# Attention and two gated layers in one kernel: in feature blocks 7 to 9 of the first layer, the middle token tile's halves get seven block products for eight

## The chip, the cores and the metric

The kernel runs on one core of a Trainium2 chip. The metric is the device time of one execution in microseconds (us); the median of 3 runs of the kernel before is 554.49 us (554.37 to 554.83). Besides these there is one profiled execution, which has a time of its own; all rows shown below come from it.

The engines are named as in the profile: PE is the matrix engine (PEld its loads of weights), DVE the vector engine, ACT the scalar engine, POOL the engine that issues accumulating transfers here, SP the one that issues plain loads and stores.

## The reference

Three stages follow one another; the output of each is the input of the next. The tokens are 2 batches of 768, 1536 in all; the model width is 512.

```python
# attention with a decaying state, 8 heads of 64
for t in range(S):
    state = gamma[None, :, None, None] * state + np.einsum('bhd,bhe->bhde', k[:, :, t], v[:, :, t])
    y[:, :, t] = scale * np.einsum('bhd,bhde->bhe', q[:, :, t], state)
x = np.ascontiguousarray(y.transpose(0, 2, 1, 3)).reshape(B * S, H * D)
# first layer: d_model 512, d_ff 1536
x = (x @ w_a) * (x @ w_b) @ w_out
# second layer: d_model 512, d_ff 2048
h = x @ w_in
out = np.maximum(0.01 * h, h) @ w_out2
```

## The kernel before

**Number format.** A float32 factor is kept as two parts, high (`h` at the end of a name) and low (`l`), and a product is three matmuls, high by high, high by low and low by high. One helper, `mm3`, issues all of them, so every matmul of the kernel stands on line 261, 262 or 263. The high part is made by a cast (CAST in the rows), the low part by a subtraction on DVE, or, for the a blocks, by a negated copy on ACT and an accumulating transfer that POOL issues.

**Tiles and blocks.** The 1536 tokens lie in three token tiles of 512: 0 and 2 are the outer ones, 1 is the middle one. The 1536 hidden features of the first layer lie in 12 blocks f of 128 features. Blocks 0 and 1 are plain. In blocks 2 to 11 (`FAST`), `seven_for_eight` takes the two outer tiles and the pair (a, b) of weight blocks together: seven block products take the place of eight, in the manner of Strassen and Winograd. They need sums of x over the outer tiles (S1 to S4, with forms `s10h` and so on), made once, and sums of the weight blocks (`ta`, `tb`, made in `sub_items` from the kept tiles of the block). The middle tile is computed plainly into the banks `pa` and `pb`: x1 by a and x1 by b, 24 matmuls of 512 columns in a block. The outer seven products go into the PSUM banks `top`, `left` and `mid`, 42 matmuls of 512 columns.

In the second layer the same is done with pairs of feature blocks, and there from the third pair on the function `seven_in_all` also gives the middle tile its seven products: its two halves of 256 tokens take the part of the outer tiles, into the half banks `intop`, `inleft` and `inmid`, 42 matmuls of 256 columns in the place of 24 of 512.

**Order of the work.** PE's stream is written out block by block. Each block is a Python generator: its first product (x10 and x11 by the next a block) is issued in the tail of the block before (`next(now)`), and its last four products stand behind that (`next(before, None)`). Behind these stand 12 matmuls of the product with w_out (`blk`, its operands called `forma`), from block 4 on.

The other engines' work is of two sorts. What a product needs at its end (a copy out of its bank, an addition) is called where it stands in the code: `s1` is the copy of the first sum out of `top` (written `h<-top`, tile h of token tile 0), `u3` the later copy out of `top` into the tile h of token tile 2, `c22` the addition of `mid` to it. All else (rounding the weights, splitting them, forming operands for w_out) lies in a queue of small items, each with a cost in microseconds that the author gave it; `pump(us)` runs items until their costs add up to `us`, `until(...)` runs them until something is there. This decides the order in which ACT and DVE get their instructions. Each engine takes its instructions in the order given.

On ACT the rounding of one weight tile begins with three instructions (the lines 330, 332 and 334, called the triple below); it ends with three on DVE.

The result of a product stays in its bank until its reader on ACT or DVE has read it, and PE may write that bank again only then. In a fast block `top` is filled by x00 and x01 with a, is read by `s1`, and is filled on by `top<-s20,tb`.

## Time and profile before

| | us |
|---|---|
| median of 3 runs | 554.49 (554.37 to 554.83) |
| the profiled execution | 553.83 |
| its span in the profile | 552.0 |
| PE busy | 547.2 (99%) |
| DVE busy | 468.3 (85%) |
| ACT busy | 394.1 (71%) |
| POOL busy | 162.5 (29%) |

The profiled execution took 0.66 us less than the median, and 1.83 us of it lie outside the span. The chain of work that ended last is PE for 96% of the span and DVE for 3%. The busy times of PE overlap from one matmul to the next (a matmul of 512 columns is shown with 0.39 us although the next begins 0.23 us later), so what counts for PE is the distance from start to start.

### The profile page before, as it was taken

To read this page: it belongs to the slowest core of one execution; us is meant where nothing else is said; L and a number is where in the kernel's file an instruction comes from. 1 tells how busy PE (TensorE), PEld (TensorE's weight loads), DVE (VectorE), ACT (ScalarE), POOL (GpSimd) and SP (SyncE) were. 2 spreads that over 40 slices of the span, in tenths; PEclk is the share of its full clock that TensorE was granted. 3 is DMA by queue.
4 is the path that set the end of the run, shared out by engine and by line. 5 is a ranking of instruction groups with operands and counts; after the bars stand their busy time and mean duration, and the time that the engine had idled before them with its cause. 6 is when DMAs were issued, how large, how long until landed. Compare 5 with 4: busy or idle time off the path is not lost.

```text
span 552.0 us, 10803 instructions
## 1 busy us (share of the span) xinstructions
PE 547.2 (99%) x3850; PEld 465.9 (84%) x3850; DVE 468.3 (85%) x1000; ACT 394.1 (71%) x821; POOL 162.5 (29%) x211
## 2 busy tenths in 40 slices
PE   9999999999999999999999999999999999999997
PEld 6878888888888888788888888888888888888886
DVE  4978968898898898899799798998989688999862
ACT  4877477787779888867768367879878777686800
POOL 3425101113232331277520320332533456700000
PEclk9999999999999999999999999999999999999999
DMA  8999835548687887899991451967979899974111
GB/s 315 354 349 242 217 96 134 155 133 207 182 260 233 247 224 249 272 299 240 237 248 39 83 110 39 245 200 230 330 222 279 259 306 259 221 168 125 58 58 57
DMA packets 51782, 112.93 MB, mean 205 GB/s; under 512 B 6224, under 2 KB 13648, under 8 KB 51728
## 3 DMA queue, kind: packets, MB, share of 16 engines
q1 hardware_dynamic: 28800, 69.16, 38.1%
q0 software_dynamic: 22784, 43.00, 35.5%
...
q14 instruction: 24, 0.20, 0.1%
...
## 4 chain that ended last, share of the span: by engine, by line
PE 96%; DVE 3%; ACT 0%; issue 0%; DVEq 0%
PE blk L262 12%; PE blk L261 12%; PE blk L263 12%; PE top L261 6%; PE top L262 6%; PE top L263 6%; PE mid L261 3%; PE pa L261 3%; PE mid L262 3%; PE mid L263 3%; PE pa L263 3%; PE pa L262 3%; PE pb L261 3%; PE pb L263 3%; PE pb L262 3%; PE left L263 1%
## 5 line engine op out<-in xcount | busy, mean ns | idle before, releaser
L262 PE MATMUL blk<-form,form 128*128 128x512 f32 (+1 forms) x224 | 75.8, 339 | 0.0
L261 PE MATMUL blk<-form,form 128*128 128x512 f32 (+1 forms) x224 | 75.6, 337 | 0.0
L263 PE MATMUL blk<-form,form 128*128 128x512 f32 (+1 forms) x224 | 75.3, 336 | 0.0
L177 DVE TENSOR_TENSOR form<-g,form 128x512 fp32r<-128x512 f32 x112 | 57.8, 554 | 1.8 <-DMA out<-c 0.9
L171 ACT CAST form<-g 128x512 fp32r<-128x512 f32 x112 | 52.5, 513 | 7.5 <-DMA g<-g 5.0
L262 PE MATMUL blk<-forma,forma 128*128 128x512 f32 (+1 forms) x168 | 56.9, 338 | 0.0
L261 PE MATMUL blk<-forma,forma 128*128 128x512 f32 (+1 forms) x168 | 56.7, 337 | 0.0
L263 PE MATMUL blk<-forma,forma 128*128 128x512 f32 (+1 forms) x168 | 56.4, 336 | 0.0
L261 PEld LDWEIGHTS blk<-form,form 128*128 128x128 f32 x224 | 42.5, 190 | 5.3
L262 PEld LDWEIGHTS blk<-form,form 128*128 128x128 f32 x224 | 42.5, 190 | 4.7
L263 PEld LDWEIGHTS blk<-form,form 128*128 128x128 f32 x224 | 42.3, 189 | 4.8
L177 DVE TENSOR_TENSOR forma<-h,forma 128x512 fp32r<-128x512 f32 x84 | 43.1, 554 | 2.2 <-ACT forma L171 0.7
L171 ACT CAST forma<-h 128x512 fp32r<-128x512 f32 x84 | 38.8, 511 | 1.4 <-DMA h<-h 1.4
L150 POOL DMA_DIRECT2D h<-h x33 | 32.9, 1151 | 12.4 <-DVE forma L177 6.0
L787 POOL DMA_DIRECT2D farg<-g x26 | 16.1, 635 | 66.9 <-ACT g L1516 42.1
L261 PEld LDWEIGHTS blk<-forma,forma 128*128 128x128 f32 x168 | 31.9, 190 | 4.0
L262 PEld LDWEIGHTS blk<-forma,forma 128*128 128x128 f32 x168 | 31.9, 190 | 3.5
L263 PEld LDWEIGHTS blk<-forma,forma 128*128 128x128 f32 x168 | 31.7, 189 | 3.6
L787 POOL DMA_DIRECT2D farh<-h x19 | 10.9, 576 | 74.8 <-DVE h L1030 50.5
L177 DVE TENSOR_TENSOR form<-wq,form 128x256 fp32r<-128x256 f32 x56 | 23.6, 421 | 7.8 <-ACT form L171 7.7
L171 ACT CAST form<-wq 128x256 fp32r<-128x256 f32 x56 | 22.7, 406 | 5.8 <-DVE wq L193 3.3
L150 POOL DMA_DIRECT2D g<-farg x22 | 22.8, 1242 | 8.9 <-DVE form L177 5.4
...
## 6 DMA issues: line engine op xcount, KB each, us to landing
...
farg<-g POOLq DMA_DIRECT2D x26, 256.0 KB, 4.5
g<-farg SPq DMA_DIRECT2D x26, 256.0 KB, 7.7
...
g<-farg POOLq DMA_DIRECT2D x20, 256.0 KB, 8.5
```

The lines of the kernel that those rows point to most:

```text
L150: queue.append((0.0, lambda piece=piece: self.nc.gpsimd.dma_start(self.A(*d[1:], j)[piece], self.A(*x1[1:], j)[piece], accum_op=ALU.add)))
L171: nc.scalar.copy(h, src)
L177: nc.vector.tensor_sub(*todo.pop(0))
L261: nc.tensor.matmul(ps, w[0], x[0], start=first, stop=False, skip_group_check=more)
L262: nc.tensor.matmul(ps, w[0], x[1], start=False, stop=False, skip_group_check=more)
L263: nc.tensor.matmul(ps, w[1], x[0], start=False, stop=last, skip_group_check=more)
L787: nc.gpsimd.dma_start(self.far[t, f], self.tiles[t, f])
```

## The change

In blocks 7, 8 and 9 of the first layer (`INNER1`) `fast(f)` calls `seven_in_all`, which now takes its inputs, its sums and the pumps as arguments. The middle tile's plain 24 matmuls of 512 columns become 42 of 256 columns there. Over the whole kernel PE loses 72 matmuls of 512 columns and gains 126 of 256.

What this needs besides:
- The sums of x over the halves of the middle tile. In block 3 four tiles `xm` are loaded from the high parts of x (SP), and the low parts are added to them by accumulating transfers (POOL), 256 KB each. Eight sums of 256 columns on DVE and four splits (a cast on ACT, `mx0h` to `mx3h`, and a subtraction on DVE) are given out over the blocks 3 to 6 by `SHARE`, and the rest, the splits of `mx2` and `mx3`, is queued when block 7 begins.
- The middle tile's ends: copies out of the half banks on ACT, four additions or products more on DVE.
- In blocks 7 to 9 only the upper half of the b block is split, since only that half is multiplied by itself. The high casts of `tb7`, `ta7`, `tb8` and `tb9` are on DVE (on ACT before).
- The stores of finished h tiles of these blocks wait in a list until the low part of the a block two further on has been issued (`landed`, `waiting`).
- The pump behind each w_out product is 0.5 in these blocks for 2.0; the pumps within a block come from `DUE` and a tuple.
- The kernel's functions `lend` and `recall` are moved, and do the same.

```diff
+DUE = {7: 2.4, 8: 1.8, 9: 1.0}
+SHARE = {3: 3, 4: 3, 5: 4, 6: 2}
+INNER1 = range(7, 10)
...
     def enqueue_split(key, keep=False, far=False):
-        part = slice(QT, TT) if key[0] == "wi" and key[1] % 2 and key[1] > 2 * INNER else slice(0, TT)
+        half = key[1] % 2 and key[1] > 2 * INNER if key[0] == "wi" else key[0] == "b" and key[1] in INNER1
+        part = slice(QT, TT) if half else slice(0, TT)
...
                 nc.gpsimd.dma_start(weights[key][1], src, accum_op=ALU.add)
+                landed.add(key)
+                while waiting:
+                    hs.send(*waiting.pop(0))
...
-                (nc.vector.tensor_copy if k[0] == "wi" else nc.scalar.copy)(weights[t][0], kept[k])
+                own = k[0] != "wi" and k[1] not in INNER1 or k[0] == "a" and k[1] > INNER1[0]
+                (nc.scalar.copy if own else nc.vector.tensor_copy)(weights[t][0], kept[k])
...
-    def seven_in_all(ka, kb, ends, inner, bent):
+    def seven_in_all(ka, kb, X, S, M, flush, ends, inner, bent, pace):
...
-        product(top, ka, 0, [y[0, 0], y[0, 1]], True, False)
+        product(top, ka, 0, [X[0, 0], X[0, 1]], True, False)
         s1(top)
         bent(1)
-        product(left, ka, 1, [y[0, 2], y[0, 3]], True, False)
+        product(left, ka, 1, [X[0, 2], X[0, 3]], True, False)
+        pump(pace[3])
         c11(left)
         left = bank("inleft")[:, 0:QT]
         product(left, ka, 1, token(X1, 0), True, False)
         mc11(left)
-        while ym:
-            spare.pop(0)[1]()
-        pump(2.7)
+        flush()
+        pump(pace[4])
         until(lambda: ta in weights and ka not in kept)
...
     def fast(f):
...
+        def mc12(ps):
+            add(um[0], um[0], ps)
+            mul(part(0), part(0), um[0])
+            half_done()
+
+        def mc21(ps):
+            nc.vector.scalar_tensor_tensor(part(1), part(1), -1.0, ps, op0=ALU.mult, op1=ALU.mult)
+            half_done()
...
+        if f in INNER1:
+            return seven_in_all(("a", f), ("b", f), x, S, inner, flush, (
+                lambda top: nc.scalar.copy(h[0, f], top),
+                lambda left: add(h[0, f], h[0, f], left),
+                uu,
+                lambda mid: nc.scalar.copy(h[2, f], mid),
+                lambda top: add(h[2, f], h[2, f], top),
+                c21, c12,
+            ), (
+                lambda ps: in_copy(part(0), ps),
+                lambda ps: add(part(0), part(0), ps),
+                muu,
+                lambda ps: in_copy(part(1), ps),
+                lambda ps: add(part(1), part(1), ps),
+                mc21, mc12,
+            ), lambda n: None, (0.4, 0.8, 0.8, 1.5, DUE.get(f, 3.6), 5.6 - DUE.get(f, 3.6)))
...
+    def inner_x():
...
+        for j in range(2):
+            for op, d, p, q in (
+                (minus_both, (2 + j, 1), (j, 1), (2 + j, 1)), (sub, (j, 1), (j, 0), (j, 1)),
+                (add, (j, 0), (j, 0), (2 + j, 1)), (add, (2 + j, 0), (2 + j, 0), (j, 0)),
+            ):
+                yield 0.42, lambda op=op, d=d, p=p, q=q: op(piece(*d), piece(*p), piece(*q))
+        for n in range(4):
+
+            def high(n=n):
+                MX[n] = slots.new(F32R, f"mx{n}h"), slots.new(F32R, f"mx{n}l")
+                nc.scalar.copy(MX[n][0], xm[n])
...
+            yield 0.05, high
+            yield 0.69, low
...
     def make_products(f):
         for n in MADE[f]:
             until(lambda: n in z.forms)
             z.product(n)
-            pump(2.0)
+            pump(0.5 if f in INNER1 else 2.0)
...
+    sums_x = list(inner_x())
     before = None
     for f in range(NBLOCK, FF1):
+        if f == INNER1[0]:
+            queue.extend(sums_x)
+        if f == NBLOCK + 1:
+            for kc in range(KC):
+                xm[kc] = slots.new(F32, f"xm{kc}")
+                nc.sync.dma_start(xm[kc], as32(x[1, kc][0]))
+                nc.gpsimd.dma_start(xm[kc], as32(x[1, kc][1]), accum_op=ALU.add)
...
+        for _ in range(SHARE.get(f, 0)):
+            queue.append(sums_x.pop(0))
```

**What stands where, first place: ACT between the last copy out of `top` in block 6 and `s1` of block 7.** In the names, a8 and b8 are weight blocks, `h26` is tile h of token tile 2 in block 6 (so `h26<-top` is `u3` of block 6), `h07<-top` is `s1` of block 7, `wo4` is a block of w_out. In the kernel before, ACT's program has this behind the two casts of `tb7` and `ta7`:

```order
L1044 COPY h26_227_1987<-top_2069 128x512
L330 ACTIVATE a8_244_2173<-raw_a8_2009 128x512
L332 ACTIVATE sl22_2174<-raw_a8_2009 128x512
L334 ACTIVATE sl22_2174<-raw_a8_2009 128x512
```

Behind that come the other two instructions of a8's triple and the triple of b8, and then, up to `s1`:

```order
L406 CAST a8h_246_2195<-a8_244_2173 128x512
L413 ACTIVATE a8l_247_2196<-a8h_246_2195 128x512
L330 ACTIVATE wo4_248_2213<-raw_wo4_2086 128x512
L332 ACTIVATE sl24_2214<-raw_wo4_2086 128x512
L334 ACTIVATE sl24_2214<-raw_wo4_2086 128x512
L171 CAST forma3_2237<-wo3_232_2035 128x256
L171 CAST forma3_2234<-h03_179_1515 128x512
L171 CAST forma3_2236<-h13_180_1516 128x256
L406 CAST b8h_249_2245<-b8_245_2189 128x512
L1040 COPY h07_241_2163<-top_2249 128x512
```

In the changed kernel the copy `h26<-top` is followed by a copy out of `intop`, which holds the first product of block 7's middle tile, and by two casts of the sums of x:

```order
L1102 COPY h26_229_2011<-top_2092 128x512
L1056 COPY h17_244_2191<-intop_2193 128x256
L1128 CAST mx2h_246_2201<-xm2_180_1521 128x512
L1128 CAST mx3h_248_2211<-xm3_181_1524 128x512
L333 ACTIVATE a8_250_2215<-raw_a8_2033 128x512
```

Behind that come again the rest of a8's triple and the triple of b8, and then:

```order
L410 CAST a8h_252_2256<-a8_250_2215 128x512
L417 ACTIVATE a8l_253_2257<-a8h_252_2256 128x512
L333 ACTIVATE wo4_254_2265<-raw_wo4_2109 128x512
L335 ACTIVATE sl24_2266<-raw_wo4_2109 128x512
L337 ACTIVATE sl24_2266<-raw_wo4_2109 128x512
L174 CAST forma3_2273<-wo3_234_2059 128x256
L174 CAST forma3_2270<-h03_182_1527 128x512
L174 CAST forma3_2272<-h13_183_1528 128x256
L1082 COPY h07_243_2190<-top_2279 128x512
```

The two casts of `tb7` and `ta7` are gone from ACT, a copy out of `intop` and the casts of `mx2` and `mx3` stand ahead of the triples, and the cast of b8 stands behind `h07<-top` now.

**Second place: DVE in block 11**, around `c22` (`h211<-h211,mid`, the addition of `mid` to tile h of token tile 2). Before:

```order
L177 TENSOR_TENSOR forma6_3035<-h10_163_1389,forma6_3035 128x256
L177 TENSOR_TENSOR forma7_3059<-wo1_201_1704,forma7_3059 128x256
L177 TENSOR_TENSOR forma7_322_3057<-h01_120_937,forma7_321_3056 128x512
L1045 TENSOR_TENSOR h211_310_2904<-h211_310_2904,mid_3012 128x512
L177 TENSOR_TENSOR forma7_3058<-h11_164_1399,forma7_3058 128x256
L177 TENSOR_TENSOR forma8_3070<-wo2_216_1853,forma8_3070 128x256
```

In the changed kernel:

```order
L354 ISA wq2_317_3129<-wq2_317_3129,sl44_3130 128x1024
L180 TENSOR_TENSOR forma6_3157<-wo0_189_1577,forma6_3157 128x256
L1103 TENSOR_TENSOR h211_308_3004<-h211_308_3004,mid_3106 128x512
L180 TENSOR_TENSOR forma6_319_3155<-h00_100_699,forma6_318_3154 128x512
L180 TENSOR_TENSOR forma6_3156<-h10_163_1389,forma6_3156 128x256
L1040 TENSOR_TENSOR h111_307_3003<-h111_307_3003,pb_3107 128x512
```

Before, one subtraction of 256 columns and one of 512 stand directly ahead of `c22`; now only one of 256 columns does, and that of 512 columns stands behind it.

## Rows read from the trace of the kernel before

**Rows 1.** Busy times in stretches: blocks 7, 9, and pair 3 of layer two.

```profile
core 0: us, PE busy (x) PEld busy (x) DVE busy (x) ACT busy (x) POOL busy (x), PEclk, DMA share, GB/s
...
155.92:172.98 17.06, 17.06 (x80) 14.23 (x79) 14.95 (x30) 13.72 (x26) 4.95 (x7) 1.00 0.78 220
...
190.04:207.10 17.06, 17.06 (x80) 14.23 (x79) 15.85 (x32) 14.34 (x28) 5.33 (x8) 1.00 0.85 234
...
345.75:362.49 16.74, 16.74 (x99) 14.75 (x98) 15.76 (x36) 14.46 (x30) 4.75 (x6) 1.00 0.80 211
```

**Rows 2.** PE in order of time, blocks 6 and 7: start, duration, instruction.

```profile
141.61 0.39 PE L261 MATMUL pa<-x12h,a6h 128*128 128x512 f32 x1
...
142.97 0.39 PE L261 MATMUL top<-s20h,tb6h 128*128 128x512 f32 x1
...
148.41 0.39 PE L261 MATMUL pb<-x12h,b6h 128*128 128x512 f32 x1
...
149.77 0.39 PE L261 MATMUL pa<-x10h,a7h 128*128 128x512 f32 x1
...
160.03 0.39 PE L261 MATMUL top<-s20h,tb7h 128*128 128x512 f32 x1
```

**Rows 3.** PE in order of time, second layer: two products of 256 columns.

```profile
348.49 0.28 PE L261 MATMUL inleft<-y10h,wi4h 128*128 128x256 f32 x1
...
349.21 0.28 PE L261 MATMUL intop<-m2h,twi5h 128*128 128x256 f32 x1
```

**Rows 4.** ACT in order of time, from `u3` of block 6 on.

```profile
148.61 0.59 ACT L1044 COPY h<-top 128x512 f32<-128x512 f32 x1 [1.52 <-PE top L263]
149.09 0.67 ACT L330 ACTIVATE a<-raw_a 128x512 f32<-128x512 f32 x1
...
152.77 0.59 ACT L406 CAST a8h<-a 128x512 fp32r<-128x512 f32 x1
...
155.77 0.38 ACT L171 CAST forma<-wo 128x256 fp32r<-128x256 f32 x1
156.05 0.92 ACT L171 CAST forma<-h 128x512 fp32r<-128x512 f32 x2
156.88 0.61 ACT L406 CAST b8h<-b 128x512 fp32r<-128x512 f32 x1
157.51 0.59 ACT L1040 COPY h<-top 128x512 f32<-128x512 f32 x1
```

**Rows 5.** PE in order of time, block 11.

```profile
234.10 0.39 PE L263 MATMUL top<-x23h,ta11l 128*128 128x512 f32 x1
234.59 0.50 PE L261 MATMUL mid<-s40h,b11h 128*128 128x512 f32 x1
```

**Rows 6.** DVE in order of time, block 11, in the same stretch.

```profile
232.73 0.42 DVE L177 TENSOR_TENSOR forma<-wo,forma 128x256 fp32r<-128x256 f32 x1 [1.02 <-ACT forma L171]
233.25 0.69 DVE L177 TENSOR_TENSOR forma<-h,forma 128x512 fp32r<-128x512 f32 x1
233.86 0.68 DVE L1045 TENSOR_TENSOR h<-h,mid 128x512 f32<-128x512 f32 x1
234.46 0.42 DVE L177 TENSOR_TENSOR forma<-h,forma 128x256 fp32r<-128x256 f32 x1
234.79 0.42 DVE L177 TENSOR_TENSOR forma<-wo,forma 128x256 fp32r<-128x256 f32 x1
```

**Rows 7.** SP's queue in block 3, in order of time.

```profile
88.37 0.33 SPq L306 DMA_DIRECT2D raw_b<-in_wab  x1
```

**Rows 8.** POOL in block 3, in order of time.

```profile
90.83 0.58 POOL L787 DMA_DIRECT2D farh<-h  x1 [10.72 <-DVE h L1030]
91.59 0.85 POOL L414 DMA_DIRECT2D a4l<-a  x1 [0.17 <-issue]
```

**Rows 9.** Transfers issued from 85 to 102 us: size, us to landing.

```profile
a4l<-a POOLq DMA_DIRECT2D x1, 256.0 KB, 5.7
```

**Rows 10.** PE in order of time, block 3: where a4's low part is used.

```profile
101.14 0.39 PE L263 MATMUL pa<-x10h,a4l 128*128 128x512 f32 x1
```

109 lines of the change are left out of this document (74 added, 35 removed).

## The prediction

> **What bounds the kernel now.** I read the page first: the chain of waits is PE almost alone. Then the table of stretches, one line per block [rows 1]: in a fast block PE is busy for the whole 17.06 us, the granted clock is 1.00, DVE is busy for 14.95 to 15.85 and ACT for 13.72 to 14.34. So no wait can be taken from PE there; a gain has to come from shorter work on PE, and a loss from a wait that PE gets. Then the instructions in order of time, of PE for the price of a matmul, of ACT and DVE for the waits that the new order makes. Between block 2 and the second layer I found one wait of PE, in block 11 [rows 5]: a matmul that follows at 234.10 + 0.23 = 234.33 begins at 234.59, 0.26 late. It needs the bank `mid`, which `c22` reads, and `c22` began only at 233.86, behind two subtractions for w_out operands [rows 6].
>
> **PE's work.** A product of six matmuls of 512 columns takes 142.97 − 141.61 = 1.36 us, 0.227 each [rows 2]; one of six with 256 columns 349.21 − 348.49 = 0.72, 0.12 each [rows 3]. For a block that is 24 × 0.227 = 5.45 against 42 × 0.12 = 5.04, 0.41 less. The second layer already has both kinds in this mixture, and a whole pair there takes 16.74 us for 17.06 [rows 1]. That is 0.32 less, with all that changing between the shapes costs, and I take it, since it is the same list of matmuls. The pieces fall into four blocks, as a block's first middle product is issued in the tail of the one before: block 6 gets 0.72 for 1.36 (−0.64), blocks 7 and 8 each −0.32, and block 9 −0.32 and +0.64, as its tail holds the plain product of block 10. In all **−0.96 us**; it would be −1.23 by the bare counts.
>
> What the trace shows against halving is the load of weights: in pair 3 the loads are busy for 14.75 us over 98, 0.15 each [rows 1], more than the 0.12 between two short matmuls. If a load could not lie beside the matmul ahead of it, 42 × 0.15 = 6.3 us would replace 5.45, a loss of 0.87 in each block. But the rows of the second layer show starts 0.12 apart with just these loads, so the term is nothing. The Trainium skill's page "TensorE: Matmul & The Clock Gate", section "Back-to-back issue gap", says that in a stream of loads and matmuls both set the spacing, with some 81 ns at 128 columns and 131 ns at 512; between these I estimate 98 ns at 256, by which 42 short ones would cost 4.1 us and 24 long ones 3.1, a loss of about 1.0 a block. The trace disagrees in both numbers (0.12 and 0.227), and the measurement decides.
>
> **ACT, and a new wait of PE in block 7.** Before, ACT goes from `u3` of block 6 (148.61) without a pause to `s1` of block 7 (157.51) [rows 4]. PE needs `s1`'s end when it fills `top` on, at 160.03 [rows 2]; `s1` lasts 0.59, so 1.9 us are to spare. In the new order a copy out of `intop` stands behind `u3`. Its product runs behind `pb` from 149.77 [rows 2] for 0.72, to 150.49. ACT began `u3` 0.20 after PE went on to the next product (148.41 to 148.61), so it begins this copy at 150.69, where before it was through with `u3` at 149.09: 1.6 us of waiting, with both triples, a8, wo and `s1` queued behind it. From there, with distances from start to start [rows 4]: the copy of 256 columns 0.28 (as the cast of 256, 155.77 to 156.05), the casts of mx2 and mx3 at 0.55 (0.83 for 512 and 256, less 0.28) 1.10, the triples of a8 and b8 3.68 (149.09 to 152.77), a8h, a8l and the triple of wo 3.00 (152.77 to 155.77), three casts for w_out 1.11 (155.77 to 156.88): 150.69 + 9.17 = 159.86. There `s1` starts, and it ends at 160.45. PE, for its part, now begins block 7 at 155.92 − 0.64 = 155.28 and wants `top` after 12 long and 12 short matmuls (`top`, `left`, `inleft`, `intop`). The long ones last 160.03 − 1.36 − 155.92 = 2.75, as before, the short ones 1.44; that is 159.47. It waits 160.45 + 0.05 − 159.47, which I take as **+1.0 us**. The distances are known to some hundredths, but ten of them in a row must hold: the bounds are 0 (the pause of 1.6 is not there, and the 1.9 now to spare do) and +2.0 (the two casts also wait, for the sums from DVE, by one more microsecond). In blocks 8 and 9 `s1` stands ahead of the casts for w_out; that takes 1.1 from the chain and leaves PE no wait there.
>
> **DVE.** Twenty-eight instructions more. In blocks 7 to 9 five of 256 columns replace one of 512 in each; besides there are eight sums of 256 columns, four splits and four casts. At 0.33 for 256 columns (234.46 to 234.79) and 0.60 for 512 (233.86 to 234.46) [rows 6] that is 3 × (1.65 − 0.60) + 8 × 0.33 + 4 × 0.60 + 4 × 0.33 = 9.5 us, less 3 × 0.27 for the half splits of b, about 8.7. It lies beside PE as long as DVE keeps up. Laying DVE's new order out between the last products of neighbouring blocks with these distances, I get 17.3 us of work in block 7, 17.3 in block 8, 15.6 in block 9, against PE's 16.74. So DVE falls back by some 1.1 us in two blocks and catches up in the third. Before, it has 17.06 − 14.95 = 2.1 us free in block 7 [rows 1], and the wait in block 7 gives it 1.0 more. I take 0, with 0 to +2.4 as bounds (+2.4: the busy time of 14.95 is 3.6% above what the same laying out gives for block 7 now, 14.43; 17.3 by that is 17.9, 1.2 over PE's 16.74 in each of two blocks).
>
> **Block 11.** With one subtraction of 256 columns ahead of it in place of one of each size, `c22` can begin at 233.25 instead of 233.86 and ends 0.6 earlier than now; PE's wait was 0.26 [rows 5, 6]. I take **−0.26**; the bounds are −0.26 and +0.3, since the new order has also more weight rounding in that block.
>
> **Transfers.** The sums' four loads stand in SP's queue ahead of the load of raw_b that is issued at 88.37, and their four accumulating transfers on POOL ahead of a store of h (90.83) and of a4's low part (91.59) [rows 7, 8]. An issue there takes 0.85, so 3.4 us for four. POOL is idle for 10.7 us ahead of 90.83, which covers them if the loads have landed. A4's low part lands 5.7 after its issue, at 97.3 [rows 9], and PE uses it at 101.14 [rows 10]: 3.8 us to spare. I take 0. The other bound: the loads are issued as late as 88.4 and land 5.7 later, at 94.1, all four issues follow, the store too, and a4's low part is issued at 98.3 and lands at 104.0: +2.9. The later stores of h in blocks 7 to 9 wait in a list, but they are brought back only when block 11 begins; 0.
>
> **Sum.** −0.96 + 1.0 − 0.26 = −0.22. On the profiled execution's 553.83 that is 553.61; this execution was 0.66 under the median, so against the runs I give 554.49 − 0.22 = **554.3 us**.
>
> **The rivals.**
> 1. *ACT is not late in block 7.* For it: ACT has 1.9 us to spare there now, and a pause ahead of the triples may be shorter than I think. Against it: the copy out of `intop` cannot begin before PE has made it. Time: 554.49 − 0.96 − 0.26 = 553.3, the full gain.
> 2. *DVE becomes the bound in blocks 7 and 8* (the other side). For it: 17.3 us of work for 16.74, and 15.85 busy already in the present block 9. Against it: its free time before. It decides from the point where DVE reads `left` or `inleft` later than PE wants the bank again. Then two blocks last 17.9 each, +2.4 in all, and block 7's wait on ACT lies inside it: −0.96 + 2.4 − 0.26 = +1.2, so 555.7.
> 3. *a4's low part comes late in block 3*: from loads that land after some 91 us on, up to +2.9 on top of the forecast, 557.2. Against it: 3.8 us to spare and an idle POOL.
> 4. *The loads of weights set the spacing of the short matmuls*: by rows +0.87 a block in place of −0.32, so 554.3 + 3.6 = 557.9. The second layer's rows speak against it. (The page named above has the same mechanism.)
>
> **Chances.** The likeliest case, a wait of about 1 us in block 7 and none elsewhere, has 0.53, with a range of its own of 553.8 to 554.8. Rival 1 has 0.18, rival 2 0.17, rival 3 0.10, rival 4 0.02. A measurement of this kernel tells about 0.2% from no change, 1.1 us: 553.4 to 555.6. Rival 1 lies on the lower edge: 0.12 faster, 0.06 the same. Rival 2 lies on the upper one: 0.10 slower, 0.07 the same. Rival 3 is slower in 0.06 and the same in 0.04. Together faster 0.12, same 0.70, slower 0.18. The range is 553.2 to 555.7: it holds the likeliest case, nearly all of rival 1 and half of rivals 2 and 3.
>
> **What would show each step.** In the profile of the changed kernel: blocks 8 and 9 at 16.74 and 17.38 us from first product to first product, block 6 at 16.42; six short matmuls in 0.72. In block 7 a wait of PE ahead of `top<-s20,tb7` on ACT's copy `h<-top`, near 1.0, and ahead of that ACT idle for 1.6 until the product in `intop`. No wait ahead of `mid<-s40,b11`. If instead PE waits in blocks 7 to 9 on DVE's reads of the half banks, DVE is the bound (rival 2); if PE waits ahead of the a4 product in block 3, the transfers are. If block 8 lasts over 17.06, the price of the short matmuls was wrong.

## The result, and the profile after

The changed kernel takes 561.47 us (median of 6 runs, 559.36 to 563.0) against 554.66 for the kernel before (6 runs, 554.28 to 555.96): a ratio of 1.0118 with an interval of 1.0094 to 1.0142. It is slower by 6.8 us, well over the 0.2% that a measurement tells. The prediction of 554.3 (553.2 to 555.7) was wrong. The profiled execution of the changed kernel took 562.31 us, with a span of 560.5 us for 552.0, and a mean granted clock of 0.997. So the profile shows 8.5 us between the kernels where the medians show 6.8, and some of the sizes below belong to this one execution; run 4 profiles the kernel a second time.

First the table of stretches of the changed kernel, with the columns of [rows 1]. The stretches are blocks 2, 6, 7, 8, 9, block 11 up to w_out, and pairs 1 and 2 of the second layer, each from first product to first product. Pairs are counted from 0 here: pair 1 is the second one, with the weight blocks wi2 and wi3, and pair 2 is the third one, which [rows 1] calls pair 3.

```profile
76.17:94.86 18.69, 16.85 (x68) 13.45 (x67) 10.66 (x21) 11.78 (x23) 4.46 (x6) 0.91 0.82 210
143.91:160.35 16.44, 16.44 (x81) 13.82 (x79) 15.97 (x34) 11.77 (x24) 4.34 (x6) 1.00 0.64 169
160.35:178.13 17.78, 17.00 (x99) 14.81 (x97) 15.64 (x34) 15.10 (x29) 2.12 (x5) 1.00 0.66 214
178.13:194.87 16.74, 16.74 (x99) 14.75 (x97) 14.98 (x34) 12.65 (x25) 5.78 (x8) 1.00 0.80 231
194.87:212.77 17.90, 17.77 (x99) 15.05 (x97) 16.41 (x34) 14.15 (x27) 4.92 (x7) 1.00 0.80 218
227.75:245.90 18.15, 17.65 (x79) 14.08 (x78) 17.47 (x38) 17.16 (x37) 6.07 (x9) 1.00 0.88 269
335.71:354.48 18.77, 17.02 (x79) 13.66 (x78) 17.77 (x37) 14.94 (x33) 0.00 (x0) 1.00 0.18 58
354.48:371.22 16.74, 16.74 (x98) 14.76 (x97) 16.02 (x36) 13.93 (x30) 4.70 (x6) 1.00 0.74 202
```

The same table of the kernel before, of the stretches that [rows 1] doesn't have (block 2, block 6, pair 1):

```profile
74.85:89.81 14.96, 14.96 (x68) 12.39 (x66) 9.60 (x19) 10.72 (x21) 0.85 (x1) 1.00 0.37 94
138.86:155.92 17.06, 17.06 (x80) 14.23 (x79) 14.57 (x29) 13.70 (x26) 4.36 (x6) 1.00 0.73 201
329.33:345.75 16.42, 16.42 (x80) 13.82 (x79) 14.31 (x31) 12.02 (x27) 0.00 (x0) 1.00 0.13 36
```

Block by block, from the first product of one to that of the next (both kernels' starts from PE in order of time), the 8.7 us between the kernels at the start of pair 2 are these:

| stretch | before | after | difference | predicted |
|---|---|---|---|---|
| up to block 2 | 74.85 | 76.17 | +1.32 | 0 |
| block 2 | 14.96 | 18.69 | +3.73 | 0 |
| block 6 | 17.06 | 16.44 | −0.62 | −0.64 |
| block 7 | 17.06 | 17.78 | +0.72 | +0.68 |
| block 8 | 17.06 | 16.74 | −0.32 | −0.32 |
| block 9 | 17.06 | 17.90 | +0.84 | +0.32 |
| block 11 to pair 1 | 107.24 | 107.96 | +0.72 | −0.26 |
| pair 1 | 16.42 | 18.77 | +2.35 | 0 |

The blocks that are left out (3 to 5 and 10) differ by 0.01 at most. Blocks 6 to 8 came out as forecast. The loss lies in places that the sum had at 0 or below: block 2, pair 1, block 11, block 9, and the stage ahead of the blocks.

**Block 2.** Views of the changed kernel: a transfer issued between 76 and 92 us, with its us to landing; the queues of SP and POOL, DVE, ACT and PE in order of time; and stretches (the wait, the matmuls behind it).

```profile
a3l<-a POOLq DMA_DIRECT2D x1, 256.0 KB, 6.3
```
```profile
79.54 0.52 SPq L1478 DMA_DIRECT2D xm<-x10h  x1
80.59 0.85 POOL L418 DMA_DIRECT2D a3l<-a  x1 [17.83 <-PE pa L266]
81.42 0.86 SPq L1478 DMA_DIRECT2D xm<-x13h  x1
```
```profile
86.89 0.43 DVE L444 TENSOR_TENSOR a<-a,b 128x256 f32<-128x256 f32 x1 [5.36 <-DMA a3l<-a]
```
```profile
88.74 0.62 ACT L464 CAST tb3h<-b 128x512 fp32r<-128x512 f32 x1 [6.34 <-DVE b L450]
89.27 0.61 ACT L464 CAST ta3h<-a 128x512 fp32r<-128x512 f32 x1
89.79 0.58 ACT L1102 COPY h<-top 128x512 f32<-128x512 f32 x1
```
```profile
88.19 0.39 PE L266 MATMUL pa<-x11h,a3l 128*128 128x512 f32 x1
90.42 0.72 PE L264 MATMUL top<-x22h,ta2h 128*128 128x512 f32 x1 [1.84 <-ACT h L1102]
90.94 0.63 PE L265 MATMUL top<-x22l,ta2h 128*128 128x512 f32 x1
91.37 0.63 PE L266 MATMUL top<-x22h,ta2l 128*128 128x512 f32 x1
```
```profile
86.00:90.42 4.42, 2.58 (x13) 1.81 (x11) 3.23 (x7) 1.68 (x4) 2.31 (x3) 1.00 1.02 178
90.42:93.93 3.51, 3.51 (x9) 2.73 (x10) 3.34 (x8) 3.51 (x6) 0.00 (x0) 0.51 0.73 129
```

Before, the same transfer and the same instruction of DVE read:

```profile
a3l<-a POOLq DMA_DIRECT2D x1, 256.0 KB, 3.7
```
```profile
82.97 0.43 DVE L437 TENSOR_TENSOR a<-a,b 128x256 f32<-128x256 f32 x1 [2.77 <-DMA a3l<-a]
```

Read it from the top. The accumulating transfer of **a3's** low part lands 6.3 us after its issue for 3.7; the four loads of `xm` were issued around it, from 79.54 to 81.42 us. DVE forms the sums of weights from it, and waits 5.36 for 2.77. ACT's queue stands in order: the casts of `tb3` and `ta3` wait for DVE, and behind them stands `u3`, the copy out of `top`, which needs no weights at all. PE wants `top` at 88.19 + 0.23 = 88.42 and gets it at 90.42: 2.0 us. Behind the wait the granted clock is 0.51, so the lower of the two levels: the matmuls start 0.43 apart for 0.227, which costs another 1.7 in this execution.

**Block 7**, PE and ACT:

```profile
164.41 0.28 PE L266 MATMUL intop<-mx1h,tb7l 128*128 128x256 f32 x1
165.46 0.50 PE L264 MATMUL top<-s20h,tb7h 128*128 128x512 f32 x1 [0.78 <-ACT h L1082]
```
```profile
155.73 0.37 ACT L1056 COPY h<-intop 128x256 f32<-128x256 f32 x1 [1.49 <-PE intop L266]
164.84 0.57 ACT L1082 COPY h<-top 128x512 f32<-128x512 f32 x1
```

The answer to [rows 4]: ACT waits 1.49 for the product in `intop` (predicted 1.6), and 9.11 later `s1` begins (predicted 9.17). PE starts 165.46 − 164.41 − 0.12 = 0.93 late, with 0.11 more at the next matmul 1.04 (predicted 1.0).

**Block 11**, PE and DVE, the answer to [rows 5, 6]:

```profile
240.12 0.39 PE L266 MATMUL top<-x23h,ta11l 128*128 128x512 f32 x1
240.97 0.50 PE L264 MATMUL mid<-s40h,b11h 128*128 128x512 f32 x1 [0.47 <-DVE h L1103]
```
```profile
239.29 0.69 DVE L354 CUSTOM_DVE_ANT_0 wq<-wq,sl 128x1024 uint16<-128x1024 uint16 x1
239.90 0.42 DVE L180 TENSOR_TENSOR forma<-wo,forma 128x256 fp32r<-128x256 f32 x1
240.24 0.68 DVE L1103 TENSOR_TENSOR h<-h,mid 128x512 f32<-128x512 f32 x1
```

`c22` stands where the order had it, behind one short subtraction, but DVE comes to it late: the rounding of wq2 still lies ahead of it, and it begins 239.29 − 227.75 = 11.5 us after the block does. Before, this row reads as follows, 229.75 − 222.09 = 7.7 us after the start of the block:

```profile
229.75 0.69 DVE L351 CUSTOM_DVE_ANT_0 wq<-wq,sl 128x1024 uint16<-128x1024 uint16 x1
```

The wait is 0.62 for 0.26.

**Block 9**, ACT:

```profile
191.29 0.62 ACT L464 CAST ta9h<-a 128x512 fp32r<-128x512 f32 x1 [3.07 <-DVE a L447]
```

ACT waits 3.07 us for a sum of weights that DVE forms late, and then works without a pause up to `s1`, which it begins at 198.79. `s1` comes late and PE waits 0.29, with the next matmul 0.40. This is the path of block 2 again, from a late DVE over ACT's queue to `top`.

**Pair 1 of the second layer.** PE, ACT and POOL of the changed kernel:

```profile
340.89 0.50 PE L264 MATMUL top<-r20h,twi3h 128*128 128x512 f32 x1 [0.94 <-ACT g L1685]
350.89 0.50 PE L264 MATMUL mid<-r40h,wi3h 128*128 128x512 f32 x1 [0.80 <-DVE g L1689]
```
```profile
331.34 0.62 ACT L838 CAST r21h<-yf 128x512 fp32r<-128x512 f32 x1 [1.67 <-DMA yf<-yc]
335.24 0.62 ACT L838 CAST r41h<-yc 128x512 fp32r<-128x512 f32 x1 [1.70 <-DMA yc<-yf]
```
```profile
313.67 0.86 POOL L1547 DMA_DIRECT2D yc<-yc  x1 [25.25 <-ACT y00h L1173]
331.87 0.86 POOL L1547 DMA_DIRECT2D yc<-yf  x1 [1.46 <-PE h L266]
```

and POOL of the kernel before:

```profile
304.78 0.86 POOL L1430 DMA_DIRECT2D yc<-yc  x1 [25.53 <-ACT y00h L1069]
321.62 0.86 POOL L1430 DMA_DIRECT2D yc<-yf  x1 [1.21 <-DVE twi2l L459]
```

The sums of y, the input of the second layer, are a chain of accumulating transfers on POOL. Its last one is issued 329.33 − 321.62 = 7.7 us ahead of pair 1 before, and 335.71 − 331.87 = 3.8 us ahead of it now. ACT waits for the sums, `s1` of pair 1 stands behind them in its queue, and PE waits. From the start of block 11 (222.09 and 227.75) the first sum of y is issued 82.7 us later before and 85.9 now, the last one 99.5 and 104.1: of the 4.6 us, 3.2 arise ahead of the sums of y and 1.4 among them.

### The profile page after: what moved, and what is told of

The parts are those of the page before. It is cut to its first block, busy times and chain, and to the rows that moved or that the text cites. A ratio compares the mean times of both kernels' runs of the same rounds, so it can differ in the third digit from the quotient of the medians.

```text
span 560.5 us, 10961 instructions
## 1 busy us (share of the span) xinstructions
PE 549.4 (98%) x3904; PEld 467.6 (83%) x3904; DVE 476.8 (85%) x1028; ACT 393.8 (70%) x824; POOL 166.4 (30%) x215
## 3 DMA queue, kind: packets, MB, share of 16 engines
HBM read 76.04 MB, written 20.71 MB: 173 GB/s over the span
## 4 chain that ended last, share of the span: by engine, by line
PE 79%; ACT 9%; DVE 7%; DMA 3%; issue 2%; SPq 0%; ACTq 0%; DVEq 0%
PE blk L265 12%; PE blk L264 12%; PE blk L266 12%; PE top L264 4%; PE top L265 4%; PE top L266 4%; PE mid L264 2%; PE mid L265 2%; PE mid L266 2%; ACT sl L335 2%; PE pa L264 2%; PE pa L266 2%; ACT sl L337 2%; PE pa L265 2%; PE pb L264 1%
## 5 line engine op out<-in xcount | busy, mean ns | idle before, releaser
L180 DVE TENSOR_TENSOR form<-g,form 128x512 fp32r<-128x512 f32 (+1 forms) x88 | 46.0, 558 | 0.3
L174 ACT CAST form<-g 128x512 fp32r<-128x512 f32 (+1 forms) x88 | 41.8, 518 | 5.5 <-DMA g<-g 5.4
L795 POOL DMA_DIRECT2D farh<-h x19 | 12.2, 780 | 50.2 <-DVE h L1044 28.5
L174 ACT CAST forma<-wo 128x256 fp32r<-128x256 f32 x42 | 16.9, 402 | 6.1 <-PE blk L266 6.1
```

Source lines behind the costliest of these rows:

```text
L174: nc.scalar.copy(h, src)
L180: nc.vector.tensor_sub(*todo.pop(0))
L795: nc.gpsimd.dma_start(self.far[t, f], self.tiles[t, f])
```

## The experiments

"Ratio" is to the kernel before on the same chip. "pair 1" is its length; it is 16.42 without a wait. The waits of PE are given as the delay of the start.

**1. The loads alone.** In the kernel before, the new transfers of block 3, whose result nobody reads:

```diff
+        if f == NBLOCK + 1:
+            for kc in range(KC):
+                xm = slots.new(F32, f"xm{kc}")
+                nc.sync.dma_start(xm, as32(x[1, kc][0]))
+                nc.gpsimd.dma_start(xm, as32(x[1, kc][1]), accum_op=ALU.add)
...
```

> The kernel before with only the four loads and four accumulating transfers of the sums' source tiles added in block 3, unused. Theory (the eight transfers share the DMA engines with a3's low part, which then lands late, ACT's casts and u3 of block 2 stand behind it, PE waits ahead of top<-x22,ta2 and its clock falls): a3's low part lands 6 us after its issue in place of 3.7, PE waits 1.5 to 2 us in block 2, the next eight or nine matmuls stand 0.43 apart, and the time rises by 3 to 4 us, to about 558. Rival (the wait comes from the new work on DVE and ACT, not from the transfers): no wait in block 2, time within 0.5 us of before.

557.42 (557.05 to 557.8), ratio 1.0052 (1.0037 to 1.0067). Transfers, DVE and PE:

```profile
xm<-x10h SPq DMA_DIRECT2D x1, 256.0 KB, 4.3
a3l<-a POOLq DMA_DIRECT2D x1, 256.0 KB, 5.8
```
```profile
87.28 0.42 DVE L437 TENSOR_TENSOR a<-a,b 128x256 f32<-128x256 f32 x1 [4.85 <-DMA a3l<-a]
```
```profile
90.81 0.50 PE L261 MATMUL top<-x22h,ta2h 128*128 128x512 f32 x1 [1.32 <-ACT h L1044]
```

The transfers alone make block 2's wait (1.5 us, and 0.2 in block 3), by the same chain. The granted clock stayed at 1.00 behind it, so the second half of the 3.73 is missing. No wait in pair 1. Of the 4.0 us by which the span of this profile is longer than before, 2.2 lie ahead of block 2.

**2. No transfers.** The changed kernel with the whole x of the middle tile formed by four additions on DVE in block 2, in place of loads and accumulates:

```diff
+    def whole_x(kc):
+        xm[kc] = slots.new(F32, f"xm{kc}")
+        nc.vector.tensor_add(xm[kc], *(as32(part) for part in x[1, kc]))
...
```

> The changed kernel without the eight transfers: DVE forms the four source tiles by additions of high and low part, two in each of its two pauses of block 2 (2.4 us in all). Theory: no wait in block 2, block 2 back to 15.0 us, 3.7 us less than the changed kernel, about 557.5 to 558; the other waits (1.0 in block 7, 0.4 in block 9, 0.6 in block 11) stay. Rival: block 2 still waits, since DVE's work is the cause: 561 or more. If the waits in the second layer's pair 1 (0.9 and 0.8) come from the late transfers too, they go as well, and the time is about 555.5; if they only vary from one execution to another, they may stay.

559.31 (558.73 to 559.65), ratio 1.0082 (1.0066 to 1.0099). Block 2 is back at 14.96 us without a wait. What is left of the loss is in the main block 7 (18.39 us long, with waits of 0.92 and, on DVE's reading of `top`, 0.38), block 9 (0.25), block 11 (0.62) and pair 1 (18.87). Both ends agree on some 2 to 3 us for the transfers (2.8 in run 1, 2.2 here); how much of that lies in block 2 varies from one execution to another.

**3. Block 7's first copy out of `intop` on DVE**, so that ACT doesn't wait there:

```diff
-                lambda ps: in_copy(part(0), ps),
+                lambda ps: (nc.vector.tensor_copy if f == INNER1[0] else in_copy)(part(0), ps),
```

> The changed kernel with one edit: in block 7 the first copy out of intop is on DVE and not on ACT, so ACT's triples do not stand behind PE's product. Theory: ACT's pause of 1.5 us ahead of that copy goes, s1 of block 7 is in time, PE's wait of 0.8 to 1.0 ahead of top<-s20,tb7 is gone, and the time falls by about 1.0 against the changed kernel, to about 560.5, unless DVE, which then waits for that product, pays it back in block 7 or 8. Rival (PE there waits for something else too): the wait stays above 0.5.

561.4 (561.16 to 564.0), ratio 1.0134 (1.0111 to 1.0158). ACT and PE:

```profile
159.11 0.62 ACT L410 CAST a8h<-a 128x512 fp32r<-128x512 f32 x1 [1.84 <-DVE a L354]
```
```profile
163.86 0.50 PE L264 MATMUL top<-s20h,tb7h 128*128 128x512 f32 x1 [0.83 <-ACT h L1082]
```

The wait stayed. ACT no longer waits at `intop`, but waits 1.84 us later on, ahead of a8's cast, for DVE's rounding of a8. Counted from the start of block 7 this rounding ends at +0.4 us here and at −0.4 in the changed kernel, where it was done 0.7 us before ACT asked for it; 0.3 of the difference is the copy that DVE now makes. Block 2 waited 1.87 here, and the clock stayed at 1.00.

**4. The changed kernel once more.**

> The changed kernel once more, unedited, for a second profile. If the waits belong to the kernel, those in block 2 (1.8, with a falling clock), block 7 (0.8), block 9 (0.3) and block 11 (0.5) come back at the same places within 0.2 us. The 0.76 us pause in the attention stage without a releaser and the waits in the second layer's pair 1 come back if they belong to the kernel, and are gone or of another size if they vary from one execution to another. Time 559 to 563.

561.82 (560.9 to 563.6), ratio 1.0135 (1.0114 to 1.0156). The same waits: block 2 1.92 with the lower clock behind it, block 7 0.92, block 9 0.23, block 11 0.62, pair 1 18.43. They belong to the kernel and not to one execution.

**5. The sums for nothing.** The changed kernel without transfers, sums and splits; the products take x's own parts in their place:

```diff
+    for n in range(KC):
+        for m, i in ((2, 0), (3, 1)) if n < 2 else ((4, 0), (1, 1)):
+            inner[m].append(tuple(part[:, i * QT:(i + 1) * QT] for part in x[1, n]))
+    sums_x = []
...
```

> The changed kernel with its seven products in blocks 7 to 9, but without the sums of x over the middle tile's halves: no transfers, no additions, no splits; the forms of x itself are used in their place, so the sums are left out of the computation. Theory (DVE's backlog: in the changed kernel DVE reads the last product of block 8 4.2 us after PE made it, where the kernel before has 1.2, and that makes c22 of block 11 late and then the chain of additions to h that ends in pair 1 of the second layer): with 5 to 6 us less work DVE's lag at block 8 falls under 2 us, the waits in pair 1 (1.2 and 1.1) go, block 11 waits 0.4 or less as before, the wait in block 2 is gone; the wait in block 7 falls to 0 to 0.3. Time 554 to 555.5, some of it from the attention stage. Rival (the waits in pair 1 come from the stores that are held back, which stay here): pair 1 waits about 2 us as in the changed kernel, 557 or more.

558.15 (557.6 to 558.77), ratio 1.0051 (1.0033 to 1.0069). Block 2 has no wait and block 7 one of 0.28, but block 11 has 0.74 and pair 1 lasts 19.27. DVE reads the last sum out of `top` of block 8 3.8 us after PE made it, for 4.2 in the changed kernel. My expectation, that DVE's lag and pair 1's waits come from the sums, fell.

**6. The sums alone**: transfers, sums and splits as in the changed kernel, their result unused, blocks 7 to 9 plain (`if f in ():` for `if f in INNER1:`), and with them the stores, the casts of `ta` and `tb` and the pumps as in the kernel before.

> The other half: the changed kernel's eight transfers, additions, casts and splits in blocks 3 to 7 as they are, their results unused, and blocks 7 to 9 with the plain middle tile, its casts on ACT, its stores at once and its pumps as before. Theory: block 2 waits 1.6 to 2 us (3.5 if the clock falls); DVE's lag at block 8 lies between that of before (1.2) and 4.2, at 2 to 3, since the periods of PE are 17.06 and it has 2 us free in each; so block 11 and pair 1 wait little: time 557 to 559. Rival (the sums on DVE alone cause the waits in pair 1): pair 1 waits 2 us here too, 560 or more.

557.7 (556.29 to 558.84), ratio 1.0048 (1.0032 to 1.0063). Block 2 waits 1.17, block 11 as before, pair 1 is 16.42. With run 5 it says: block 2 is from the sums' transfers, and block 11 and pair 1 are from the seven products or from what came with them (held stores, casts on DVE, pumps). Of these three, run 7 takes back the casts and run 9 the stores.

**7. Less on DVE and another order on ACT**: as run 2, with the casts of `tb` and `ta` on ACT again, all splits ahead of block 7, and the copy out of `intop` directly ahead of `s1`:

```diff
-        ms1(in_top)
+        if ka[0] != "a":
+            ms1(in_top)
...
+        if ka[0] == "a":
+            ms1(in_top)
...
```

> Mended version: no transfers (DVE adds high and low part in the pauses of block 2), the casts of tb7, ta7, tb8 and tb9 back on ACT, all four splits given out before block 7, the pump behind block 6's w_out product 0.5, and the copy out of intop put directly ahead of s1, so that ACT does not wait for it ahead of the triples. Theory: no wait in block 2; in block 7 ACT's pause is gone and PE waits at most 0.3; DVE's lag at block 8 about 2.5 and the waits in pair 1 half of what they were: 556 to 557.5, 2 to 3 us under the version with the additions alone (559.3). Rival (DVE's lag is set by the total of its work and not by where it stands): lag 4 us, the waits in pair 1 unchanged, 558.5 or more.

559.41 (558.76 to 559.96), ratio 1.0071 (1.005 to 1.0093). PE in block 7:

```profile
161.45 0.28 PE L266 MATMUL intop<-mx1h,tb7l 128*128 128x256 f32 x1
161.57 0.40 PE L264 MATMUL top<-s20h,tb7h 128*128 128x512 f32 x1
```

Block 7's wait is gone (16.78 us). But block 4 has 0.7, block 9 0.72 (now at the copies out of `intop`), block 11 1.0, and pair 1 lasts 19.09.

**8. The kernel before, profiled once more.**

> The kernel before, unedited, for a second profile. If the time of the attention stage belongs to the program, block 2 begins at 74.9 again within 0.2 us; if it varies between executions, at another time, up to 77 as in the kernel with the loads alone.

554.4. Its block 2 begins at 75.42, where the other profile has 74.85; from there to pair 2 the blocks are of the same length.

**9. Stores of h at once**, not held until the a block's low part has been issued (`if f in () and ...`):

> The changed kernel with one edit: the stores of h of blocks 7 to 9 are issued at once and not held back. Rival (the held stores shift the later chain of additions to h and so cause the waits in pair 1 of the second layer): the waits in pair 1 (1.2 and 1.1 us together with what follows them) go, time 559.5 or less. Theory (DVE's lag in blocks 8 to 11 causes them): they stay within 0.4 us, DVE's lag at blocks 9 to 11 stays 3.6, 2.8 and 3.5, time 560.5 to 562.5.

561.32 (559.7 to 562.11), ratio 1.0109 (1.0082 to 1.0135). Block 11's wait at `mid` is gone and pair 1 is 17.45, but a10's low part lands 7.6 us after its issue (4.2 in the changed kernel) and PE waits for it:

```profile
204.37 0.50 PE L266 MATMUL pa<-x10h,a10l 128*128 128x512 f32 x1 [0.77 <-DMA a10l<-a]
```

In the product with w_out 1.7 us of new waits follow. These waits are why pair 1 got shorter: PE comes to it 1.8 us later (counted from block 7), while the last sum of y is issued 171.7 us after the start of block 7, as in the changed kernel (171.5). PE's wait for a10 also lets DVE catch up (its lag at block 9 is 2.6 for 3.6), which fits that block 11's wait is gone. So the list of held stores keeps a10 in time; that it makes the sums of y late is not shown.

**10. Run 5 with three of five inner additions left out** as well (`lambda ps: None` for two `add`, and the one on `um` dropped).

> The kernel without the sums of x (their forms replaced by those of x) and, besides, without three of the five additions on DVE by which a middle tile's inner product ends (two additions to h and one to um, 256 columns each, some 1.1 us in a block): these are left out of the computation too. Theory: DVE gets back its free time in blocks 7 to 9, its lag at block 11 falls from 3.5 towards 2.2, the wait in block 11 falls from 0.74 towards 0.37 and those in pair 1 from 2.8 in all to under 1: time 555 to 556.5 against 558.15 with the additions. Rival (the place of the weight rounding in the order, not the amount of DVE's work): lag at block 11 over 3.2, pair 1 waits 2.5 or more, 557.5 or more.

557.91 (556.58 to 558.1), ratio 1.005 (1.0033 to 1.0067). Pair 1 lasts 18.89. So much less work on DVE in blocks 7 to 9 changes the median by 0.2 us. In the profile block 11's wait falls to 0.40 (0.74) and the sums of y end 2.0 us earlier, but PE comes to pair 1 1.6 us earlier too, so its wait hardly changes. DVE's lag at block 11 is 3.1.

**11. The kernel before with some 4 us of additions on DVE**, meant for the end of the blocks (`for _ in range(5): nc.vector.tensor_add(idle, ...)` in block 9).

> The kernel before with only a delay of DVE: a cast and five additions of 512 columns into a scratch tile, about 4 us, at the start of block 10's part of DVE's program. PE's program is that of before, with no seven products in the middle tile. Theory (a late DVE at the end of the first layer is enough): c21 of block 9 and 10 is read 3 to 4.5 us late, block 11 waits 0.3 to 0.7 more, and pair 1 of the second layer waits 1.5 to 3 us where the kernel before waits nothing: time 556.5 to 558.5. Rival (the waits in pair 1 need the new products or the held stores): no wait in pair 1, within 0.7 of before.

558.91 (557.26 to 559.86), ratio 1.0066 (1.004 to 1.0092).

```profile
197.44 0.50 PE L261 MATMUL top<-s20h,tb9h 128*128 128x512 f32 x1 [2.68 <-ACT h L1040]
```

It hit `c21` of block 8, so PE waited for 2.9 us at once in block 9, and DVE was on time again by block 11. It says nothing on the end of the blocks; it does show that DVE has no 4 us to spare here.

**12. Seven products in blocks 5 to 7** (`INNER1 = range(5, 8)`, otherwise like run 7).

> A version for gain: the seven products in blocks 5 to 7 in place of 7 to 9, the source tiles by additions on DVE in the pauses of block 2, all sums and splits in blocks 3 and 4 where DVE has most free time, the casts of ta and tb on ACT, the copy out of intop directly ahead of s1. Theory: the same 0.96 us less on PE, and DVE has blocks 8 to 11 in the old order to catch up: lag 1.2 at block 8 and 2.2 at block 11 as before, waits in pair 1 gone, one or two waits of 0.3 in blocks 3 to 5: 554 to 555.5, no slower than before. Rival (DVE's work cannot be hidden anywhere in the first layer): lag 3 us or more at block 8, waits in pair 1, 557 or more.

561.79 (560.62 to 563.19), ratio 1.0122 (1.0097 to 1.0148). Pair 1 is 16.91, near to the length before, but blocks 3 to 5 wait for 5.9 us together, 4.0 of it for ACT's copies out of `intop`. The waits moved; no gain.

**13. Two tiles of wq not rounded** by DVE in block 11 (3.3 us of its work left out):

> The changed kernel without the six instructions (3.3 us) by which DVE rounds the two weight tiles wq1 and wq2 in block 11, just ahead of the operands for w_out; the rounding is left out of the computation, all else stays. Theory (DVE is late with the operands for w_out at the end of the first layer, so the chain of additions to h starts late, and pair 1 of the second layer waits for what comes out of it): the wait in block 11 falls from 0.7 to 0.3 or less, pair 1 waits under 1 us in place of 2 to 2.3, time 558.5 to 559.8 against 561.5. Rival (the waits in pair 1 have another cause, such as the order of the h tiles): pair 1 waits 1.8 or more.

559.93 (559.13 to 561.19), ratio 1.0092 (1.0066 to 1.0117). Block 11's wait at `mid` is gone: without this rounding ahead of `c22` DVE is in time. Its lag at block 11 is 2.3 us, about that of before (2.2), and yet pair 1 is still 18.73.

**14. The kernel before with 2.5 us of additions on DVE in block 11** (`if f == FAST[-1]`, behind the reads of `mid` and `pb`).

> The kernel before with a cast and three additions into a scratch tile on DVE, 2.5 us, put in block 11 behind the reads of mid and pb, ahead of the operands for w_out from the third on. PE's program is that of before. Theory (a late DVE at this place is enough): no wait of PE up to there beyond the 0.37 of before, and in pair 1 of the second layer waits of 1 to 2.3 us together, time 555.8 to 557.3. Rival (a late DVE there is made up in the stage of w_out): no wait in pair 1, within 0.5 us of before.

554.79 (554.2 to 555.56), ratio 0.9999 (0.999 to 1.0008). Pair 1 has no wait. DVE's lag at block 11 is 4.7 us here, more than in the changed kernel, and it is made up; the theory that this lateness alone makes pair 1 wait fell.

**15. The kernel before with DVE's order of the changed kernel in block 11** (`forma6`'s two parts that read h, and `forma7`, behind `c22`):

```diff
-        pump(3.3)
+        pump(3.3 if ka != ("a", FF1 - 1) else 3.3 - 2.2)
...
-        pump(0.7)
+        pump(0.7 if ka != ("a", FF1 - 1) else 0.7 + 2.2)
```

> The kernel before with only the order of VectorE in block 11 changed to what the changed kernel has there: of the first operand set of the second half of the output projection (forma6) the part of wo stays ahead of c22, its two parts that read h (and the next set, forma7) stand behind c22, which waits for u3. Theory (order): GpSimd's chain of additions onto h begins when the read of h00 is done, so it begins some 2 to 4 us later than the 9.59 us after the start of block 11 that the kernel before shows; the sums of y come late and TensorE waits 0.5 to 2 us in pair 1 of layer 2, while the wait of 0.37 in block 11 goes or stays: 554.5 to 556.5. Rival (the sums of y have room whatever the order): no wait in pair 1, 554.0 to 554.6.

554.42 (553.79 to 555.53), ratio 0.9993 (0.9983 to 1.0002). The first addition onto h of this stage begins 12.57 us after block 11 does, for 9.59, and yet pair 1 has no wait. Block 11's wait (0.26, with the matmul behind it 0.37) went:

```profile
234.48 0.39 PE L263 MATMUL top<-x23h,ta11l 128*128 128x512 f32 x1
234.70 0.39 PE L261 MATMUL mid<-s40h,b11h 128*128 128x512 f32 x1
```

The order alone isn't it either.

**16, 17 and 18. The opposite order in run 13, in the changed kernel and in run 7**: `forma6` ahead of `c22` (`3.3 + 2.2` and `0.1` in the two pumps of run 15).

> The changed kernel without the rounding of wq1 and wq2 (as e13_two_unrounded, 559.93), and with forma6 and two parts of forma7 ahead of c22 on VectorE in block 11, as the kernel before has them. Theory (order): the first addition onto h lies 9.6 to 11 us after the start of block 11, where e13 had 12.9, and the waits of pair 1 (2.25 together) fall below 0.8: 557.9 to 558.8. Rival (what makes the sums of y late lies elsewhere, in a sum of x or in the late loads): pair 1 still above 1.8, 559.5 to 560.3.

> The changed kernel with nothing else but forma6 and one part of forma7 ahead of c22 on VectorE in block 11. Theory (order): the first addition onto h comes at 10 to 12 us after the start of block 11 instead of 14.1, pair 1 falls from 2.2 to below 1.0, and the wait in block 11 grows by at most 0.8, as VectorE does 1.5 us more ahead of c22: 559.8 to 561. Rival (VectorE's lag, not its order): what is won in pair 1 is paid in block 11 and at the output projection, where the waits grow by 1.5 or more: 561 to 562.5.

> e7_less_dve (559.41: the sums formed without transfers, the twisted casts on ScalarE, block 7's copies in another order) with the same move of forma6 ahead of c22. Theory (order): pair 1 falls from 2.6 to below 1.0: 557.6 to 558.6, still over the kernel before, by the waits of blocks 4, 9 and 11 and by the start of the blocks. Rival: the waits move into block 11 and the output projection, 559 to 560.

16: 560.22 (559.58 to 561.41), ratio 1.0106 (1.0091 to 1.0121). 17: 562.26 (561.6 to 565.32), ratio 1.0151 (1.0122 to 1.018). 18: 559.77 (558.98 to 560.52), ratio 1.009 (1.0074 to 1.0107). Pair 1 falls from 18.73 to 16.90 and from 18.77 to 17.25 in the first two, and only from 19.09 to 18.77 in the third. The time falls in none: in 17 the wait in block 11 is 1.22 (0.62 in the changed kernel), with 0.57 ahead of it, so that PE is late for pair 1 by itself, and in the other two the difference to the run without the move lies within the scatter.

**All runs together on pair 1.** "Sums end" is the issue of the last transfer of the sums of y, "PE comes" the start of pair 1, both from the trace and counted from the first product of block 7; "lead" is the difference.

| kernel | sums end, us | PE comes, us | lead, us | pair 1, us |
|---|---|---|---|---|
| 6 | 165.3 | 173.4 | 8.1 | 16.42 |
| 11 | 168.5 | 176.4 | 7.9 | 16.41 |
| 14 | 165.6 | 173.4 | 7.8 | 16.41 |
| before | 165.7 | 173.4 | 7.7 | 16.42 |
| 15 | 166.0 | 173.0 | 7.0 | 16.42 |
| 8 | 166.7 | 173.4 | 6.8 | 16.41 |
| 1 | 166.7 | 173.4 | 6.7 | 16.42 |
| 16 | 169.2 | 175.3 | 6.1 | 16.90 |
| 12 | 168.6 | 174.6 | 6.05 | 16.91 |
| 17 | 170.9 | 176.6 | 5.7 | 17.25 |
| 9 | 171.7 | 177.2 | 5.5 | 17.45 |
| 4 | 171.5 | 175.7 | 4.2 | 18.43 |
| 13 | 170.8 | 174.7 | 3.9 | 18.73 |
| after | 171.5 | 175.4 | 3.8 | 18.77 |
| 18 | 172.0 | 175.8 | 3.8 | 18.77 |
| 2 | 172.5 | 176.3 | 3.75 | 18.87 |
| 10 | 170.1 | 173.8 | 3.7 | 18.89 |
| 7 | 171.6 | 175.1 | 3.5 | 19.09 |
| 3 | 172.1 | 175.4 | 3.4 | 19.20 |
| 5 | 172.1 | 175.4 | 3.3 | 19.27 |

Pair 1 has no wait down to a lead of 6.7 us, and below about 6.5 it loses nearly as much as the lead does. So the end of this chain of transfers, against PE's arrival, sets pair 1 in all of these kernels. The lead can grow in two ways, though. Against the changed kernel it grows wholly in run 9, and by two thirds in run 17, because PE was held up earlier, which gains nothing. The sums themselves end earlier by 2.4 us in run 16, 1.4 in run 10, 0.7 in run 13 and 0.6 in run 17, of the 5.8 us between the two kernels. (Run 12 has its seven products in other blocks.)

## Why the prediction was wrong

Two steps failed. The term "Transfers, 0" looked at the wrong transfer: a3's low part landed 2.6 us later than before, and block 2 lost 3.7 us in the profile. And the working ended at block 11, where the second layer then lost 2.35 us in pair 1. Together with smaller misses this goes beyond every rival, the highest of which stood at 557.9.

- **PE's work, −0.96: right.** Block 6 16.44 (16.42 forecast), block 8 16.74 (16.74), short matmuls 0.12 apart (161.45 to 161.57 in run 7), as in [rows 3]. By an estimate from the figures of the page "TensorE: Matmul & The Clock Gate" of the Trainium skill (section "Back-to-back issue gap") a block would have lost 1.0 us; block 8 got 0.32 shorter, so the trace disagrees with it again.
- **ACT in block 7, +1.0: right, 1.04.** The rows show the path: ACT's pause of 1.49, and 9.11 us without a gap up to `s1`. In run 7 another order on ACT together with less work on DVE takes the wait away, and in run 5, where ACT has two casts less there, it falls to 0.28. Run 3 shows a second bound just behind it: with ACT's pause gone, DVE's rounding of a8 is late, so that change alone gives nothing.
- **Transfers, taken as 0: wrong, +3.73 in the profile; the largest error there.** I followed what stands *behind* the new transfers in the queues of SP and POOL, and priced a4's low part. The one that suffered, a3's, was issued ahead of POOL's four and between SP's, and was in flight beside them: 3.7 us to landing became 6.3. I also had the loads go as late as 88.4 us, and they went at 79.54 to 81.42. I counted issue slots and not what was in flight. The page "DMA: Bandwidth & Descriptors" of the Trainium skill says, under "Issuing engines are not separate DMA queues", that transfers started by different engines run on the same 16 DMA engines and interleave; the two landing times fit it, and I had not weighed it. The chain from there (DVE, ACT's casts, `u3` behind them, `top`) had some 0.6 us to spare, so 2.0 us of wait came out, and the lower clock made it 3.7. Runs 1, 2 and 6 show that the transfers are the cause, and all twenty profiles agree: a3's low part lands after 3.4 to 4.2 us in the eleven without these transfers, and block 2 has no wait; it lands after 5.5 to 6.3 in the nine with them, and PE waits 1.2 to 2.0. In block 2 the clock fell in only two of the nine, both profiles of the changed kernel itself; of its six executions two have a mean clock of 0.996 or 0.997 and four of 0.999 or more. Where it does not fall, block 2 costs 1.3 to 2.0 us, less than the 2.35 of pair 1. Rival 3 had the mechanism with the wrong tile, and 2.9 as its most.
- **DVE "falls back by some 1.1 us in two blocks and catches up in the third": wrong in the second half.** The amount of work was right: DVE is busy for 476.8 us in all, 8.5 more than before (8.7 forecast). Measure its lag as the start of `c21` less the end of the last matmul into `top`. In blocks 7 to 11 it was 0.04, 1.2, 0.04, 1.0, 2.2 before, and 1.8, 4.2, 3.6, 2.8, 3.5 in the changed kernel. For block 8 of the changed kernel these two rows give 197.12 − (192.57 + 0.39) = 4.16:

```profile
192.57 0.39 PE L266 MATMUL top<-x23h,ta8l 128*128 128x512 f32 x1
```
```profile
197.12 0.68 DVE L1044 SCALAR_TENSOR_TENSOR h<-h,top 128x512 f32<-128x512 f32 x1
```

  From one `c21` to the next, close to how the forecast laid its order out, DVE is busy for 17.2, 17.3 and 15.9 us up to those of blocks 7, 8 and 9 (17.3, 17.3 and 15.6 forecast), but these stretches last 19.4, 19.1 and 17.4 us. I had counted its work, and not the 1.5 to 2.1 us of each in which it stands idle. So it fell back by 2.4 us in block 8 alone and made up only 0.6 in block 9. But the form in which rival 2 had it, blocks of 17.9 with DVE as the bound, did not come either: block 8 is at 16.74. The lag passes under PE until something that PE needs waits for it.
- **Block 11, −0.26: wrong, +0.65.** I took the start of `c22` from the order, with DVE as early as before; more weight rounding in the block was in the bound of +0.3 alone. The rounding of wq2 ahead of `c22` begins 11.5 us after the start of the block, 7.7 before, and without this rounding (run 13) the wait is gone. Run 15 shows the term itself right: where DVE is on time, this order does take the wait away. Of the +0.72 in the table, 0.65 is what the waits here grew by: 0.73 at `mid` and 0.29 ahead of `top<-s30,tb11`, for 0.37 before, each with the matmul behind it.
- **Block 9, +0.5 over the forecast.** `s1` is late there too, by 0.40 with the matmul behind it; I had ruled such a wait out because it stands ahead of the casts for w_out. The row of ACT shows that DVE's lag got there first: ACT waited 3.07 us for DVE's sum of weights. No run tests this wait by itself.
- **The second layer was not in the sum: +2.35.** I ended the working at block 11. That the chain of sums of y ends late is shown by the table of all runs: 165.3 to 166.7 us after the start of block 7 where these blocks are plain (168.5 in run 11, where PE itself was 2.9 late), and 170.1 to 172.5 with seven products in blocks 7 to 9 (169.2 in run 16). What makes it late is shown in part. It needs neither the sums of x with their transfers (run 5: 172.1), nor the held stores (run 9: 171.7), nor the casts on DVE (run 7: 171.6); the changed pumps were not tested by themselves. Left out, three additions at the ends of the middle tile are worth 2.0 (run 10), the rounding of wq1 and wq2 0.7 (run 13), and DVE's order in block 11 1.6 beside that (run 16) but 0.6 in run 17 and nothing in run 18. A DVE that is late in block 11 does not suffice (run 14), nor does its order there (run 15), and the sums end late even where DVE's lag at block 11 is as before (run 13). How the rest comes about stays open.
- **The stage ahead of the blocks, +1.32: open.** Nothing in it was edited. The kernel before begins block 2 at 74.85 and 75.42 in two profiles, the changed one at 76.17 and 76.04, and run 1 at 77.09, with small waits in other places each time. Over all twenty profiles it begins at 74.85 to 75.44 in the seven that have neither the sums of x nor their transfers, and at 75.45 to 77.09 in the thirteen that have one or both. So it may not be scatter alone; no run shows how instructions that come later would act on this stage.

No version that was run beats the kernel before. Run 7 takes the waits of blocks 2 and 7 away, but what is left or new in it, in block 4, block 9, block 11, the product with w_out and pair 1, exceeds the 0.96 us that the change can win.
